# P V in 64x32 tiles over the live quarters, in two parts around a score set: a fused transformer block on one Trainium2 core

## The chip, the cores and the metric

The kernel runs on one core of one Trainium2 chip. The metric is the device time of one execution in microseconds (us), lower is better. The kernel before takes 324.31 us, the median of three runs (324.24 to 324.77).

## The reference, cut to what matters

One transformer block on 2048 tokens of width 640. Attention has 32 heads of 20 channels; every token sees itself and the 255 tokens before it. The second half is a gated MLP of width 1536. Both halves have a layer norm whose scale and shift, and a gate on the output, come from a small conditioning vector.

```python
mod = (_silu(c) @ w_mod).reshape(c.shape[0], 6, 1, -1)      # sa, ca, ga, sb, cb, gb
h = _layernorm(x) * (1 + ca) + sa
qkv = (h @ wqkv)                                            # 32 heads of 20, three times
scores = einsum('bhqd,bhkd->bhqk', q, k) * 20 ** -0.5
mask = (i - j >= 0) & (i - j < 256)
o = einsum('bhqk,bhkd->bhqd', softmax(where(mask, scores, -1e9)), v)
x = x + ga * (o @ wo)
h = _layernorm(x) * (1 + cb) + sb
x = x + gb * ((sigmoid(h @ w_gate) * (h @ w_up)) @ w_down)
```

## The kernel before, in words

The tokens are cut into 8 chunks `a` of 256 queries, each of two blocks of 128. For a chunk, the keys that can be live lie in four blocks of 128: two of the chunk before (`kb` = -2, -1) and two of its own (0, 1). The heads stand in 8 groups of 4; a step of attention, called (a, q) here, takes four groups `k` at once, so a chunk has two steps.

In a step TensorE (PE) first makes scores, keys on the partitions and queries on the columns. One *score set* fills the one PSUM tile S (4 banks of 512 columns, bank `j` for one of four heads). ScalarE (ACT) turns it into bf16 with one exponential (L981) in a tile E of SBUF; PE can write the next set only when that is done, since there is one S. GpSimd (POOL) then sets what is not live to zero with `affine_select` (L947). When all sets of a step are masked, PE does P V for the step: the *burst*, into two PSUM banks X. Column 20 of each head's V holds ones, so the sum of the softmax comes with it. VectorE (DVE) turns X (L1112, twice), divides, and at a chunk's second step turns the result into `oT`. Then come the output projection `wo`, the residual, the second layer norm, a DMA that transposes, the modulation, and the MLP (`wg`, `wu`, `wd`). Q and K get their transposed form `QT`, `KT` through DMAs as well (L769): projection on PE, copy out of PSUM into `stg` on ACT or DVE, DMA on SyncE's queue (SP).

Not every quarter of the scores is live. A quarter is 64 keys by 64 queries; of the 32 in a step's four key blocks 20 are, 8 of them cut by the diagonal. Two layouts stand beside each other:

- chunks 3 to 7 (merged): four main sets, one for each `k`, made of 20x64 tiles (half a key block each) so that two half blocks share a column, and one edge set for all `k` in 20x128 tiles. Five sets a step. `spread` masks and copies parts of a main set into the edge tile F, which takes two slots of E.
- chunks 1 and 2 (`WHOLE`): six sets a step of whole key blocks, in 20x128 tiles, masked in place. Chunk 0 has three sets a step.

A burst is 64 matmuls of 128x32 tiles (128 keys, 32 columns of V): for each `k` two of 256 columns and two of 128, each for four heads side by side in the array. It is issued together with a score set, straight ahead of it, as one operation (`both_of`).

Every instruction is an `op` with an engine, its reads and writes. The order on each engine, and which buffer an operation gets, stand as a list of numbers in the file (`PLAN`, `SLOTS`), made ahead of time; between engines the program waits by semaphores that follow from reads and writes. Engines run their lists strictly in order. Dense matmuls go through L634, tiled ones through L635.

Of the kernel before, what the change touches and what calls it, by code (L numbers as in the profile page):

```python
# [19 lines left out]
NG = H // 4  # L20
# [3 lines left out]
VW = 22  # L24
# [281 lines left out]
def c_pe(n):  # L306
# [132 lines left out]
MW = 64  # L439
NE = 8  # L440
ESI = 2
WHOLE = (1, 2)
WM1 = (3, 5)
AFTER = 1
NOW = 1
# [10 lines left out]
def build(nc, A_x, A_wqkv, A_wo, B_x, B_w_gate, B_w_up, B_w_down, c, w_mod, out, S=2048):  # L456
    NCH = S // CH
    P = Prog(nc)
    A = P.op
# [867 lines left out]
```

## Time and profile before

| | |
|---|---|
| median of three runs | 324.31 us |
| the profiled execution | 324.32 us, of which the span is 322.6 us |
| PE busy | 316.8 us, 98% of the span |
| ACT, DVE, POOL busy | 214.6, 199.9, 193.9 us |
| granted TensorE clock | full in all 40 slices |
| exponentials (L981) | 80, 1878 ns each |
| masks (L947) | 234, 149.3 us for the group that the page lists |

The span is what the profile covers; 1.7 us of the execution lie outside it. A row of the chain reads: start in us, duration, engine, tile written, line, number of instructions. The time of a row runs to the start of the next, so it holds what it costs to change over to the next kind of matmul. In a timeline row the duration runs to the end of the last instruction, which for pipelined matmuls lies well after the start of the next row; differences of starts are the better measure there. `128*32` is a tile of 128 rows and 32 columns in the array, `20*64` one of 20 rows and 64 columns.

### The profile page before, as it was taken

The page shows a single profiled execution, that of the slowest core. Times are in us where ns is not written, and L with a number is a line of the kernel's source. Part 1 is how long each engine was busy: PE and PEld are TensorE (multiplying, and loading weights), DVE is VectorE, ACT ScalarE, POOL GpSimd, SP SyncE. Part 2 cuts the span into 40 slices and gives each one's busy share as a digit, 9 for nine tenths or more (in the row PEclk, how much of TensorE's full clock was granted, in tenths as well). Part 3 has the DMA queues.
Part 4 walks back from the last instruction along what each step waited for, and adds up shares of the span by engine and source line. Part 5 has one row for each costly group of instructions (what it writes and reads, how often), then busy time and mean ns, then how long its engine had stood idle before and what let it go on. Part 6 is the DMA issues. An engine that isn't in the chain of part 4 may idle for free.

```text
span 322.6 us, 11139 instructions
## 1 busy us (share of the span) xinstructions
PE 316.8 (98%) x4766; PEld 230.9 (72%) x4766; DVE 199.9 (62%) x424; ACT 214.6 (67%) x220; POOL 193.9 (60%) x334
## 2 busy tenths in 40 slices
PE   6999999999999999999999999999999999999997
PEld 2666656577776677766787667876788777877885
DVE  6796999677585545685557454676438453485422
ACT  1489999997798787859785858684768557200320
POOL 4338679788788596969393839585672836601000
PEclk9999999999999999999999999999999999999999
DMA  7999799999912343308250211420400021012111
GB/s 231 374 332 199 198 258 206 184 273 317 210 40 41 103 92 48 62 3 130 55 114 4 35 35 48 102 43 2 122 6 4 2 43 43 2 41 43 41 43 42
DMA packets 64619, 33.61 MB, mean 104 GB/s; under 512 B 49082, under 2 KB 63034, under 8 KB 64570
## 3 DMA queue, kind: packets, MB, share of 16 engines
q1 hardware_dynamic: 63744, 31.92, 42.3%
q10 hardware_dynamic: 826, 0.98, 0.9%
q8 instruction: 37, 0.61, 0.8%
q14 instruction: 12, 0.10, 0.1%
HBM read 18.35 MB, written 2.62 MB: 65 GB/s over the span
## 4 chain that ended last, share of the span: by engine, by line
PE 89%; POOL 4%; ACT 3%; DVE 2%; DMA 1%; issue 1%; SPq 0%; ACTq 0%; DVEq 0%; POOLq 0%
PE M L634 74%; PE S L635 8%; PE M L635 7%; POOL E L947 3%; ACT E L981 2%; DMA x<-in_A_x_dram 1%; DVE x L762 1%; DVE st L741 1%; POOL st L749 1%; POOL st L747 0%; ACT QT L664 0%; DVE hT L823 0%; DVE st L743 0%; ACT hT L777 0%; SPq L533 0%
## 5 line engine op out<-in xcount | busy, mean ns | idle before, releaser
L947 POOL TENSOR_SCALAR_AFFINE_SELECT E<-E 128x256 bf16<-128x256 bf16 (+2 forms) x234 | 149.3, 667 | 52.2 <-ACT E L981 34.5
L981 ACT ACTIVATE E<-S 128x2048 bf16<-128x2048 f32 x80 | 150.2, 1878 | 42.3 <-PE S L635 41.6
L634 PE MATMUL M<-h2T,wu 128*128 128x256 bf16 x480 | 66.4, 273 | 0.0
L634 PE MATMUL M<-h2T,wg 128*128 128x256 bf16 x480 | 65.8, 273 | 0.0
L1225 DVE SCALAR_TENSOR_TENSOR hh<-sig,M 128x512 bf16<-128x512 f32 x48 | 32.4, 681 | 43.8 <-ACT sig L1223 31.6
L634 PE MATMUL M<-wd,hh 128*128 128x320 bf16 (+2 forms) x396 | 56.4, 295 | 0.0
L634 PEld LDWEIGHTS M<-h2T,wu 128*128 128x128 bf16 x480 | 45.7, 98 | 8.1 <-issue 1.6
L634 PEld LDWEIGHTS M<-h2T,wg 128*128 128x128 bf16 x480 | 45.5, 98 | 8.3 <-issue 1.5
L634 PEld LDWEIGHTS M<-wd,hh 128*128 128x128 bf16 x396 | 37.0, 98 | 14.9 <-issue 1.4
L1223 ACT ACTIVATE sig<-M 128x512 f32<-128x512 f32 x48 | 28.4, 596 | 26.1 <-PE M L634 25.0
L635 PE MATMUL S<-QT,KT 20*64 20x64 bf16 (+5 forms) x1600 | 33.3, 231 | 0.5
L1112 DVE STREAM_TRANSPOSE T<-M 128x512 f32<-128x512 f32 x32 | 21.7, 698 | 12.2 <-PE S L635 10.0
L741 DVE BATCH_NORM_STATS2 st<-x 128x6 f32<-128x320 bf16 x64 | 28.3, 477 | 1.1 <-DMA x<-in_A_x_dram 0.8
L635 PEld LDWEIGHTS S<-QT,KT 20*64 20x64 bf16 (+1 forms) x1600 | 15.2, 99 | 18.4 <-ACT E L981 9.8
L634 PE MATMUL M<-wk,hT 128*128 128x320 bf16 x160 | 28.2, 300 | 0.0
L634 PE MATMUL M<-wv,hT 128*128 128x320 bf16 x160 | 28.0, 300 | 0.0
L634 PE MATMUL M<-wo,oT 128*128 128x320 bf16 x160 | 26.5, 300 | 0.0
L634 PE MATMUL M<-wq,hT 128*128 128x320 bf16 x160 | 26.0, 300 | 0.2 <-DVE hT L823 0.2
L1244 DVE TENSOR_TENSOR x<-M,x 128x320 bf16<-128x320 f32 (+2 forms) x33 | 15.4, 478 | 15.1 <-PE M L634 14.5
L1179 DVE TENSOR_TENSOR x<-M,x 128x320 bf16<-128x320 f32 x32 | 15.3, 487 | 13.6 <-PE M L634 13.0
L747 POOL TENSOR_SCALAR st<-st 128x2 f32<-128x2 f32 (+1 forms) x17 | 4.0, 233 | 32.7 <-DVE st L743 31.7
L635 PEld LDWEIGHTS M<-E,V 128*32 128x32 bf16 x960 | 19.9, 97 | 4.5 <-issue 2.2
(81 smaller groups left out, 298.9 us busy)
## 6 DMA issues: line engine op xcount, KB each, us to landing
x<-in_A_x_dram SPq DMA_DIRECT2D x11, 320.0 KB, 3.6
wd<-in_w_mod_dram SPq DMA_DIRECT2D x6, 320.0 KB, 5.0
wd<-in_B_w_down_dram SPq DMA_DIRECT2D x4, 480.0 KB, 5.3
out_dram<-x SPq DMA_DIRECT2D x5, 320.0 KB, 2.6
wg<-in_B_w_gate_dram SPq DMA_DIRECT2D x2, 576.0 KB, 6.9
wu<-in_B_w_up_dram SPq DMA_DIRECT2D x2, 576.0 KB, 6.2
wu<-in_w_mod_dram SPq DMA_DIRECT2D x1, 960.0 KB, 10.5
wq<-in_A_wqkv_dram SPq DMA_DIRECT2D x2, 400.0 KB, 6.7
```

What stands on the lines that cost most here:

```text
L634: return e.matmul(o, l, r, start=st, stop=sp, skip_group_check=True)
L635: return e.matmul(o, l, r, start=st, stop=sp, tile_position=tp, skip_group_check=True)
L741: A("dve", lambda e, g, bi=bi, j=j: e.bn_stats(v(bi * 12 + j * 6, 6), src[bi].ap[:, j * 320:(j + 1) * 320]), 0.48, reads=[src[bi].r()], wr ...
L747: A("pool", lambda e, g, lo=lo, w=w: e.tensor_scalar(v(28 + lo, w), var()[:, lo:lo + w], EPS, None, op0=ALU.add), 0.2, reads=[st.r(("m", b ...
L749: A("pool", lambda e, g, lo=lo, w=w: e.tensor_tensor(v(30 + lo, w), v(28 + lo, w), mhalf[:, 0:w], op=ALU.pow), 0.71, reads=[st.r(("v", lo) ...
L947: return lambda e, eng: e.affine_select(dst(), src(), pattern=pattern, compare_op=ALU.is_ge, fill=0.0, base=base, channel_multiplier=mul)
L981: A("act", lambda e, eng: e.activation(dst(), src(Sp.ap), ACT.Exp, scale=SM_SCALE), 1.876, reads=[Sp.r()], writes=[E.r()], prio=3, tag=f"e ...
L1112: A("dve", lambda e, g, h=h: e.transpose(T1.ap[:, 512 * h:512 * h + 512], X[h].ap), 0.694, reads=[X[h].r()], writes=[T1.r(h)], prio=3.5, t ...
L1179: A("dve", lambda e, g, ps=ps, bi=bi, half=half: e.tensor_tensor(x1[bi].ap[:, half * 320:half * 320 + 320], ps.ap[:, 0:320], x1[bi].ap[:, ...
L1223: A("act", lambda e, g, pg=pg, sg=sg: e.activation(sg.ap[:], pg.ap[:], ACT.Tanh, scale=0.5), c_act(512), reads=[pg.r()], writes=[sg.r()], ...
L1225: A("dve", lambda e, g, pu=pu, sg=sg, f0=f0: e.scalar_tensor_tensor(out=hh.ap[:, f0:f0 + 2, :], in0=sg.ap[:].rearrange("p (a b) -> p a b", ...
L1244: A("dve", lambda e, g, ps=ps, bi=bi, c0=c0, n=n: e.tensor_tensor(x1[bi].ap[:, c0:c0 + n], ps.ap[:, 0:n], x1[bi].ap[:, c0:c0 + n], op=ALU. ...
```

## The change

1. **P V in 64x32 tiles over live quarters alone.** A piece is now half a key block (64 keys, partitions 0 to 63 or 64 to 127), and takes only the queries for which one of its quarters is live: for each `k` and head 1, 2, 3 or 4 quarters, 20 in all. A burst has 128 matmuls, of 256, 192, 128 and 64 columns, 32 of each. Matmuls of the lower and of the upper half alternate, lower with `k` 0 and 1 while upper has 2 and 3, so that the two write to different PSUM banks.
2. **In two parts.** `burst_halves` issues two operations; the second, with lower and upper swapped, waits on the first by a semaphore (`fence`). In the new order a score set, and at times dense matmuls, stand between the two.
3. **Merged sets in chunks 1 and 2 too** (`WHOLE = ()`): five sets a step in place of six, so 76 sets in all and not 80. The edge set is made of 20x64 tiles as well.
4. **Masks in place.** The edge tile takes one slot of E. Of a step's 18 masks 14 are on 64 partitions and four on 128. Where a mask on partitions 64 to 127 follows another instruction of POOL, or is followed by one, POOL waits for the one before (`part`); there are five such masks in a step.
5. **The order** is new from some 33 us on, on all engines, and with it which of ACT, DVE and POOL does some copies and modulations.

```diff
-WHOLE = (1, 2)
+WHOLE = ()
...
-    def score_set(a, q, si, tag, prods, low, E, dst, src, more=()):
+    def score_set(a, q, si, tag, prods, E, dst, src):
...
-            def both_of(e, eng):
-                pv(e, eng)
-                return sc(e, eng)
...
+        if pend and si == AFTER:
+            alone(*pend.pop(0))
...
+    def half_mask(a, E, key, g, t0, m, off):
+        hi, kind = key[:2] == "hi", key[2] == "A"
+        p0, p1 = (64, 128) if hi and kind else (0, 128) if hi else (0, 64)
+        ap = lambda: E.ap[p0:p1].rearrange("p j (t c) -> p j t c", c=g)[:, :, t0:t0 + m, off:off + 64]
+        mask(a, 256 * m, select(ap, ap, [[0, 4], [0, m], [-1 if kind else 1, 64]], -1 if kind else 64 * hi, 1 if kind else -1), [E.r()], [E.r(key)],
+             part="hi" if p0 else None)
...
     def edge_set(a, q, si):
-            prods += [(k, -2, 0, 128, 0, 64, 128 * k), (k, 1, 0, 128, 192, 64, 128 * k + 64)]
+            prods += [(k, 1, 0, 64, 128, 128, 128 * k), (k, -2, 64, 64, 0, 128, 128 * k)]
...
     def main_set(a, q, k, si):
-        prods = [(k, 1, 0, 64, 128, 64, 192), (k, -2, 64, 64, 64, 64, 256), (k, -1, 0, 64, 0, 192, 0), (k, 0, 64, 64, 64, 192, 320),
-                 (k, 0, 0, 64, 0, 256, 256), (k, -1, 64, 64, 0, 256, 0)]
+        prods = [(k, -2, 0, 64, 0, 64, 448), (k, 1, 64, 64, 192, 64, 256), (k, -1, 0, 64, 0, 192, 256), (k, 0, 64, 64, 64, 192, 320),
+                 (k, 0, 0, 64, 0, 256, 0), (k, -1, 64, 64, 0, 256, 0)]
+        half_mask(a, E, "loA", 64, 6, 2, 0)
+        half_mask(a, E, "hiB", 64, 4, 2, 0)
+        half_mask(a, E, "loB", 64, 0, 1, 0)
+        half_mask(a, E, "hiA", 64, 3, 1, 0)
...
-    def spread(a, q, k, E, F, fa):
...
+    def burst_halves(a, q, pieces):
+        o = None
+        for ph in range(2):
+            line = []
+            for p0 in (0, 64):
+                at = 0
+                for k in (2 * (ph ^ (p0 > 0)), 2 * (ph ^ (p0 > 0)) + 1):
+                    for p in sorted((p for p in pieces if p[0] == k and p[2] == p0), key=lambda p: KBO[p0].index(p[1])):
+                        line.append((at, p0, p))
+                        at += p[4]
+            line.sort(key=lambda x: x[:2])
...
+                        ins = mm(e, X[bank].ap[32 * j:32 * j + 32, oc:oc + n * 64], V[2 * a + kb].ap[p0:p0 + 64, h * VW:h * VW + 32],
+                                 ap(j), ph == 0 and (bank, j) not in seen, True, tp=(p0, 32 * j))
...
+            o = A("pe", pv, 0.55, reads=list(rd), writes=[x.r() for x in X], prio=8, lat=0.2, tag=f"pv{ph}_{a}", fence=o)
+        return X
...
+    KBO = {0: (0, -1, -2, 1), 64: (-1, 0, 1, -2)}
```

Three places show how the order moves, all on PE. The first is the first score set of chunk 1. `wk,hT1` is the K projection of chunk 1, `wv,hT1` its V projection, `KT0` and `KT1` are the transposed keys of chunks 0 and 1. Before:

```order
L634 MATMUL M<-wk,hT1 128x320 x5
L634 MATMUL M<-wv,hT1 128x320 x10
L635 MATMUL S0<-QT1,KT1 128x256 x4
L635 MATMUL S0<-QT1,KT0 128x256 x4
L634 MATMUL M<-grow,ident 128x160 x4
L634 MATMUL M<-wv,hT1 128x320 x5
```

And after:

```order
L636 MATMUL M<-wk,hT1 128x320 x5
L636 MATMUL M<-wv,hT1 128x320 x17
L636 MATMUL M<-grow,ident 128x160 x4
L636 MATMUL M<-wv,hT1 128x320 x3
L637 MATMUL S0<-QT1,KT0 64x64 x4
L637 MATMUL S0<-QT1,KT1 64x64 x4
L637 MATMUL S0<-QT1,KT0 64x192 x4
L637 MATMUL S0<-QT1,KT1 64x192 x4
```

The set stood behind ten matmuls and read the first key block of `KT1` alone; it now stands behind 24 and reads both, the second of which comes from the `wk` row at the top.

The second place is the first burst of chunk 1. Before:

```order
L634 MATMUL M<-wv,hT 128x320 x8
L635 MATMUL M<-E,V 32x256 x16
L635 MATMUL M<-E,V 32x128 x16
L635 MATMUL M<-E,V 32x256 x16
L635 MATMUL M<-E,V 32x128 x16
L635 MATMUL S<-QT,KT 128x256 x8
L634 MATMUL M<-wq,hT 128x320 x7
```

And after:

```order
L637 MATMUL M<-E,V 32x192 x8
L637 MATMUL M<-E,V 32x64 x8
L637 MATMUL M<-E,V 32x128 x8
L637 MATMUL S<-QT,KT 64x128 x32
L636 MATMUL M<-wq,hT 128x320 x13
L637 MATMUL M<-E,V 32x256 x8
L637 MATMUL M<-E,V 32x192 x8
L637 MATMUL M<-E,V 32x64 x8
```

One run of 64 matmuls ahead of a score set has become two runs of 64 (here the end of the first and the head of the second), with the edge set of the next step and 13 dense matmuls between.

The third place is in the same chunk, where two score sets stand close together. Before, behind the first burst:

```order
L635 MATMUL S<-QT,KT 128x128 x16
L634 MATMUL M<-wq,hT 128x320 x13
L634 MATMUL M<-wv,hT 128x320 x2
L635 MATMUL S<-QT,KT 128x256 x8
```

And after, ahead of it:

```order
L637 MATMUL S<-QT,KT 64x64 x8
L637 MATMUL S<-QT,KT 64x192 x8
L637 MATMUL S<-QT,KT 64x256 x8
L636 MATMUL M<-wq,hT 128x320 x11
L637 MATMUL S<-QT,KT 64x64 x8
```

Between one set and the next stood 15 dense matmuls; now there are 11.

More of the change, by code (lines that the diff above doesn't have):

```diff
@@ L966, in score_set, with mask @@
                 rd[QT[a].r((bi, q))] = 1
-        md = 3 if low else 1
-        now = pend.pop(0) if pend and si == AFTER else None
-        if now is None:
-            last["s"] = [A("pe", sc, 0.243, reads=list(rd), writes=[Sp.r()], prio=10, lat=0.2, tag=f"{tag}{a}",
-                           extra=last["s"], mode=md, hold=[E, *more])]
-        else:
-            pa, pv, pd, prd, X, hold = now[0]()
-            def both_of(e, eng):
-                pv(e, eng)
-                return sc(e, eng)
-            rd.update(prd)
-            last["s"] = [A("pe", both_of, pd + 0.09 + 0.243, reads=list(rd), writes=[Sp.r(), X[0].r(), X[1].r()], prio=10, lat=0.2,
-                           tag=f"pvs{pa}", extra=last["s"], mode=2, mout=md, hold=[E, *more, *hold, *X])]
-        A("act", lambda e, eng: e.activation(dst(), src(Sp.ap), ACT.Exp, scale=SM_SCALE), 1.876,
-          reads=[Sp.r()], writes=[E.r()], prio=3, tag=f"exp{a}", hold=more)
-        if now is not None:
-            now[1]()
-    def mask(a, n, fn, reads, writes, hold=()):
-        A("pool", fn, c_pool(n), reads=reads, writes=writes, prio=5, tag=f"mask{a}", hold=hold)
+        if pend and si == AFTER:
+            alone(*pend.pop(0))
+        last["s"] = [A("pe", sc, 0.243, reads=list(rd), writes=[Sp.r()], prio=10, lat=0.2, tag=f"{tag}{a}", extra=last["s"], hold=[E])]
+        A("act", lambda e, eng: e.activation(dst(), src(Sp.ap), ACT.Exp, scale=SM_SCALE), 1.876,
+          reads=[Sp.r()], writes=[E.r()], prio=3, tag=f"exp{a}")
+    def mask(a, n, fn, reads, writes, part=None):
+        A("pool", fn, c_pool(n) + (0.2 if part else 0.0), reads=reads, writes=writes, prio=5, tag=f"mask{a}", part=part)
     def first_sets(q):
@@ L1027, in edge_set @@
[L1027 to L1028 removed]
+        E = Tile(p_E, f"E{a}_{q}_4")
         prods = []
         for k in range(4):
[L1031 to L1035 removed]
@@ L1061, in sets @@
         if a in WHOLE:
-            return whole_sets(a, q)
-        F, fa, Es = None, None, []
+            return in_halves(whole_sets(a, q))
+        F, Es = None, []
         for si in range(5):
             if si == ESI:
-                F, fa = edge_set(a, q, si)
-                done = range(len(Es))
+                F = edge_set(a, q, si)
             else:
                 Es.append(main_set(a, q, len(Es), si))
-                done = [len(Es) - 1] if F is not None else []
-            for k in done:
-                spread(a, q, k, Es[k], F, fa)
@@ L1073, in sets @@
         out = []
+        fr = [F.r(), F.r("loB"), F.r("hiA")]
         for k, E in enumerate(Es):
[L1075 to L1080 removed]
@@ new lines, in sets, with in_halves, pv @@
+        return out
+    LIVE = {(-2, 0): (0, 1), (-1, 0): (0, 3), (0, 0): (0, 4), (1, 0): (2, 4), (-2, 64): (0, 2), (-1, 64): (0, 4), (0, 64): (1, 4), (1, 64): (3, 4)}
+    def in_halves(pieces):
+        out = []
+        for k, kb, u, n, ap, rs in pieces:
+            for p0 in (0, 64):
+                q0, q1 = LIVE[kb, p0]
+                out.append((k, kb, p0, q0, q1 - q0, lambda j, ap=ap, p0=p0, a0=q0 - 2 * u, a1=q1 - 2 * u: ap(j)[p0:p0 + 64, 64 * a0:64 * a1], rs))
+        return out
+    def burst_halves(a, q, pieces):
+        X = [Tile(p_M, f"O{a}_{q}x"), Tile(p_M, f"O{a}_{q}y")]
+        X[0].mate, X[1].mate = X[1], X[0]
+        o = None
+        for ph in range(2):
+            line = []
+            for p0 in (0, 64):
+                at = 0
[4 more added lines that the diff above has]
+            line.sort(key=lambda x: x[:2])
+            def pv(e, eng, ph=ph, line=line):
+                ins = None
+                seen = set()
+                for _, p0, (k, kb, _, u, n, ap, _) in line:
+                    bank = k // 2
+                    oc = (k % 2) * 256 + u * 64
+                    for j in range(4):
+                        h = NG * j + 4 * q + k
+                        ins = mm(e, X[bank].ap[32 * j:32 * j + 32, oc:oc + n * 64], V[2 * a + kb].ap[p0:p0 + 64, h * VW:h * VW + 32],
+                                 ap(j), ph == 0 and (bank, j) not in seen, True, tp=(p0, 32 * j))
+                        seen.add((bank, j))
+                return ins
+            rd = {}
+            for _, _, p in line:
+                rd.update(dict.fromkeys(p[6]))
+                rd.update(dict.fromkeys(V[2 * a + p[1]].r(h) for h in range(2)))
+            o = A("pe", pv, 0.55, reads=list(rd), writes=[x.r() for x in X], prio=8, lat=0.2, tag=f"pv{ph}_{a}", fence=o)
+        return X
@@ L1102, in burst @@
             rd.update(dict.fromkeys(rs))
-        for kb in range(-2 if a else 0, 2):
-            rd[V[2 * a + kb].r(0)] = 1
-            rd[V[2 * a + kb].r(1)] = 1
-        hold = list(dict.fromkeys(r.tile.mate for r in rd if r.tile is not None and r.tile.mate is not None))
-        return a, pv, sum(n for _, _, _, n, _, _ in pieces) * 128 / 2400.0 * 1.04 + 0.02, rd, X, hold
+        for kb in range(2):
+            rd[V[kb].r(0)] = 1
+            rd[V[kb].r(1)] = 1
+        A("pe", pv, sum(n for _, _, _, n, _, _ in pieces) * 128 / 2400.0 * 1.04 + 0.02, reads=list(rd), writes=[X[0].r(), X[1].r()],
+          prio=8, lat=0.2, tag=f"pvs{a}", hold=X)
+        return X
     def norm(X, Tn, oT, a, q):
@@ L1124, in norm, with alone @@
                   0.03 + 0.305 * (t1 - t0), reads=[Tn.r(0), Tn.r(1)], writes=[oT.r(t0 // 2)], prio=4, tag=f"tr2_{a}")
+    KBO = {0: (0, -1, -2, 1), 64: (-1, 0, 1, -2)}
     pend = []
-    def later(a, q, pieces, close):
-        made = []
-        def first():
-            made.append(burst(a, q, pieces))
-            return made[0]
-        return first, lambda: close(q, made[0][4])
-    def alone(first, then):
-        pa, pv, pd, prd, X, hold = first()
-        A("pe", pv, pd, reads=list(prd), writes=[X[0].r(), X[1].r()], prio=8, lat=0.2, tag=f"pvs{pa}", mode=2, hold=hold + X, extra=last["s"])
-        then()
+    def alone(a, q, pieces, close):
+        close(q, (burst_halves if a else burst)(a, q, pieces))
     def attention(a):
@@ L1152, in attention @@
             if a < NOW:
-                alone(*later(a, q, pieces, close))
+                alone(a, q, pieces, close)
             else:
-                pend.append(later(a, q, pieces, close))
+                pend.append((a, q, pieces, close))
     def add_pair(x, pss, prio, tag):
```

51 lines of the change are left out of this document (17 added, 34 removed), and 203 rows, old and new, of the table PLAN.

## The prediction

> **What bounds the kernel now.** First the shares and the chain on the page, then PE's own waits.
>
> ```profile
> PE 316.8 (98%) x4766; PEld 230.9 (72%) x4766; DVE 199.9 (62%) x424; ACT 214.6 (67%) x220; POOL 193.9 (60%) x334
> PE 89%; POOL 4%; ACT 3%; DVE 2%; DMA 1%; issue 1%; SPq 0%; ACTq 0%; DVEq 0%; POOLq 0%
> PE M L603 <- DMA c_row<-in_c_dram: 2.3, 1, 2.3
> PE M L635 <- POOL E L947: 0.2, 1, 0.2
> PE M L634 <- DVE hT L823: 0.2, 1, 0.2
> PE M L634 <- DVE x L762: 0.2, 1, 0.2
> ```
>
> PE is busy 98%, and of its 2.9 us of waits 2.3 are the start. So PE's own work sets the end: what PE is spared counts in full, what it newly waits for too, and time saved on ACT counts for nothing by itself. The sum is made against the profiled execution, 324.32 us (span 322.6 and 1.7 around it), 0.01 from the median of 324.31. About 0.2% (0.65 us) is what a measurement of this kernel can tell from no change.
>
> **What PE's work costs.** A dense stretch of the timeline, then pieces of the chain.
>
> ```profile
> 303.16 1.25 PE L634 MATMUL M<-h2T,wg 128*128 128x256 bf16 x10
> 304.25 0.82 PE L634 MATMUL M<-h2T,wu 128*128 128x256 bf16 x6
> ...
> 56.99 0.33 PE S L635 x8
> ...
> 106.84 0.36 PE S L635 x24
> 107.20 2.14 PE M L634 x15
> 109.35 0.34 PE S L635 x32
> ...
> 121.82 1.43 PE M L635 x64
> 123.25 0.36 PE S L635 x24
> ```
>
> Ten matmuls of 256 columns start in 304.25 - 303.16 = 1.09 us, so 0.109 for 256 columns; by columns 0.136 for 320, 0.082 for 192, 0.055 for 128, 0.027 for 64. Tiled matmuls run side by side, four or eight a round, or these rows could not be so short: 64 matmuls of a burst, 32 of 256 and 32 of 128 columns, are 16 rounds of four, 8 x 0.109 + 8 x 0.055 = 1.31 of the 1.43. A main set (8 matmuls each of 64, 192 and 256) is 0.027 + 0.082 + 0.109 = 0.22 of 0.36; an edge set, 8 rounds of 64, 0.22 of 0.34; a whole set, 2 rounds of 256, 0.22 of 0.33; 15 dense matmuls 2.04 of 2.14. What is left, 0.10 to 0.14, is the price of changing to the next kind of tile: 0.10 from dense, 0.11 to 0.12 from four in a round, 0.14 from eight.
>
> **The change, part by part.**
>
> *P V over live quarters.* One half has, lower beside upper, two groups `k` of one round each of 256, 192, 128 and 64 columns, eight matmuls in a round: 2 x 0.273 = 0.55. With a change at 0.12 (the burst's row, the same weights) to 0.14 (the main set's, eight in a round) it is 0.67 to 0.69, a burst of two 1.34 to 1.38 in place of 1.43. I take 0.67, since the main set's first round of 64 columns has no counterpart here: 14 bursts x 0.09 = -1.2 us, between -0.7 and -1.3. No 64x32 tile stands in the trace; the nearest thing with eight in a round is the main set. The Trainium skill, "TensorE: Matmul & The Clock Gate", Part 3, gives tiles side by side some 4 ns each after the first; as an estimate from that, eight end 16 ns later than four, which puts a half at 0.68 and the sum 0.4 us higher. The main set's 0.14 lies on that side.
>
> *Score sets.* Chunks 1 and 2 had 24 sets x 0.33 = 7.9; now 16 main x 0.36 + 4 edge x 0.34 = 7.1: -0.8. The ten edge sets of chunks 3 to 7 become four rounds of 128 in eights, 0.22 + 0.12 to 0.14: 0 to +0.2, taken as 0 with their own row.
>
> *Changes back from dense.* Counted over the order's rows, dense work is left 78 times where it was 81: -0.3. That a half is now a piece of its own is in its 0.67.
>
> So PE's work: -1.2 - 0.8 - 0.3 = -2.3 us.
>
> *The first score set of chunk 1.* It now reads both key blocks of its chunk.
>
> ```profile
> 32.26 1.52 PE L634 MATMUL M<-wv,hT 128*128 128x320 bf16 x10
> 32.50 0.45 DVE L665 CAST stg<-M 128x320 bf16<-128x320 f32 x1
> 32.98 1.23 SPq L769 DMA_TRANSPOSE KT<-stg  x1
> 33.71 0.40 PE L635 MATMUL S<-QT,KT 20*128 20x256 bf16 x8
> 34.04 0.45 PE L634 MATMUL M<-grow,ident 128*128 128x160 bf16 x4
> 34.33 0.84 PE L634 MATMUL M<-wv,hT 128*128 128x320 bf16 x5
> ...
> DMA to landing us min/median/max: 3.6/3.6/3.6
> ```
>
> The last row is that of the tile KT in this stretch. The second block's projection ends at 32.26, its copy at 32.95, its transpose is issued at 32.98 and lands at 36.6. None of this moves. PE does 20 `wv` matmuls (2.7) and the `grow` ones (0.29) first and reaches the set at 32.26 + 3.0 + 0.1 = 35.4. It then stands until 36.6: +1.25 us (0.9 if the landing is a few tenths quicker, 1.5 if copies slip). Behind it on PE stands everything; next in line is `wk` of chunk 2, which waits here although its input is there.
>
> *Sets closer than the exponential.*
>
> ```profile
> 52.12 0.36 PE S L635 x8
> 52.48 0.02 issue
> 52.51 1.89 ACT E L981
> 54.39 0.05 issue
> 54.44 0.40 PE S L635 x16
> ```
>
> With one S, a set can start 54.44 - 52.48 = 1.96 after the one before ended. Between the two sets of the third place lie 11 x 0.136 + 0.10 = 1.60: +0.36. By the same count three more pairs in the new order are 0.1 short, against two in the old one (this row, and one more): together +0.25 net.
>
> *Masks.* Of 252 masks of chunks 1 to 7, 196 are on 64 partitions, which no row shows.
>
> ```profile
> L947 POOL TENSOR_SCALAR_AFFINE_SELECT E<-E 128x512 bf16<-128x512 bf16 x112 | 70.8, 650 | 9.7 <-DVE wo L1272 3.0 <-ACT E L981 1.2 <-DVE x L762 1.0
> L947 POOL TENSOR_SCALAR_AFFINE_SELECT E<-E 128x1024 bf16<-128x1024 bf16 x40 | 44.9, 1135 | 16.4 <-ACT E L981 13.2 <-ACT V L664 1.7 <-DVE wd L1206 0.8
> L947 POOL TENSOR_SCALAR_AFFINE_SELECT E<-E 128x256 bf16<-128x256 bf16 x80 | 32.9, 424 | 25.7 <-ACT E L981 19.5 <-DVE x L762 2.2 <-DVE h2T L778 1.9
> L749 POOL TENSOR_TENSOR st<-st,mhalf 128x2 f32<-128x2 f32 x15 | 10.7, 712 | 0.9
> L754 POOL TENSOR_SCALAR st<-st 128x1 f32<-128x1 f32 x6 | 2.1, 366 | 0.4
> L1206 POOL TENSOR_TENSOR wd<-wd,gbc 128x640 bf16<-128x640 bf16 x5 | 6.9, 1394 | 1.8 <-DVE hT L778 1.2 <-DMA wd<-in_B_w_down_dram 0.5
> 280.00:322.60 42.60, 40.35 (x392) 32.39 (x389) 20.19 (x40) 6.37 (x11) 1.54 (x4) 1.00 0.14 40
> 101.44 3.86 POOL E L947 x5
> 105.30 0.04 issue
> 105.34 1.50 PE M L635 x64
> ```
>
> By columns, a step's masks cost 8 x 0.650 + 8 x 0.424 + 2 x 1.135 = 10.9, as merged steps did; a whole step's 9.7, so +4.5 us in chunks 1 and 2. Each of 70 masks on the upper half brings two waits of POOL on itself. L749, which always waits for POOL's instruction ahead, sat idle 0.9 / 15 = 0.06 for it: 140 x 0.06 = 8.4 us. Five `wd` products leave POOL (-7.0) and two of `wo` come (+2.8 at the same price). POOL goes from 194 to some 203, 63% of the span, and is no bound. What matters is a burst that comes before its last mask, as at 105.34 (PE waited 0.2). I counted for each burst the PE work between its last scores and itself against exponential (1.89) and masks in POOL's order: before, margins run from -0.3 to +1.1; after, from -0.4 to +4.3, with four below zero in place of two, while five have over 2 us. The nearest row is the one wait of 0.2, so I take 0, between -0.3 and +2 (a wait of 0.2 for each POOL change in the four tight bursts).
>
> *The fence and X.* The second half waits for the first. A score set (0.36) or dense work stands between in all but one burst, and covers it as the change of tile does; where the halves touch, the price is at least nothing and at most a few tenths: +0.1. X's two banks stay taken longer by what stands between, and dense chains have the other two; the tightest reuse of a bank by count is the same before and after.
>
> *Moved off the path.*
>
> ```profile
> wd<-in_w_mod_dram SPq DMA_DIRECT2D x1, 480.0 KB, 5.2
> ...
> 281.78 38.58 PE M L634 x324
> ```
>
> ACT loses four exponentials and 13 modulations or so, DVE gains some 5 us on 200; both stay under 65%. On SP the loads for the second conditioning product stand ahead of `wo`, `wg` and the fifth `x`; the product comes at about 43 us, and its last load, issued near 36, lands by 41.2 with the 5.2 of this load's row: 0, with 2 us in hand. The tail behind the last burst is 38.6 us of dense work, and is as long by count in the new order.
>
> New waits less the 0.2 at 105.34, where the margin is now 0.8: 1.25 + 0.25 + 0 + 0.1 - 0.2 = +1.4.
>
> **Sum:** 324.32 - 2.3 + 1.4 = 323.4 us.
>
> **The rivals.**
>
> *The waits eat it.* For this speaks that gain and new waits are of one size: with 0.14 for the change (+0.5) and four tight bursts late by 0.2 each, or 1.5 for the first set, the sum is 324.3. Against: the old order runs margins as tight almost without a wait. Not faster from 0.3 us more than I took.
>
> *POOL late (slower).* The place is the masks' last stretch ahead of a burst. If POOL has to run empty at each change of half, the price of one may be not 0.06 but the whole of a small instruction, L754's 0.37: 140 x 0.3 = 43 us more, POOL near 246 us, nearly all before 280 us, since behind it POOL works 1.54 us (the windows' row, its fifth busy time). A burst's last 11 masks hold about six changes, 1.8 us late, less margins of under 1 in eight of 14 bursts: 8 x 1.2 = +10, so 333. It decides from about 0.2 a change (0.8 x 4 bursts = +3, some 326). Only L749's 0.06 speaks against it.
>
> *The two halves take turns.* Each half then costs 0.55 more: 28 x 0.55 = +15, so 339. The main set's 0.36 for three rounds of eight speaks against it: there four row tiles write four banks at once. The Trainium skill, "TensorEngine Tiling (Array Packing)", Gotcha 1, says that row tiles must not use one PSUM bank at the same time and that software has to see to it; by that rule the halves run together as long as lower and upper are in different banks, as the order of `k` makes them, and this 339 is what it would cost otherwise. No run here shows it for accumulating matmuls.
>
> *More than forecast.* With the landing early, no mask late, and the main set's own change price at 0.12, 324.3 - 2.7 + 0.9 = 322.5.
>
> **How the numbers follow.** Forecast and "more" together 0.50 (321.4 to 323.7; the low end is PE's -2.3 with -0.6 more and no new wait), waits eat it 0.28 (323.7 to 324.95), POOL late 0.15, turns 0.04, other losses 0.03. Faster 0.51, with 0.01 of the rest; same 0.27; slower 0.22. The range runs from 321.4 to 325.6, where a weak case of POOL late still lies; a fifth is left out.
>
> **What would show it.** Right: halves of 64 matmuls at 0.65 to 0.70 in the chain, 0.36 for main sets, a PE wait of about 1.2 us near 36 us at a score set, released by a DMA to KT, PE busy near 315. Wrong: a half at 1.2 (turns); rows "PE M <- POOL E" of several tenths each, many times, and POOL waiting on POOL (POOL late); no wait near 36 us would leave a gain of over 2.

## The result, and the profile after

The changed kernel takes 336.85 us (median of four runs, 335.95 to 338.27) against 324.54 beside it: 1.038 times as long, 95% interval 1.034 to 1.043. The forecast was 323.4, and 325.6 was the top of its range. The profiled execution took 336.06 us.

The page of the changed kernel, its shares, its instruction queue (packets, MB, share) and its chain; the queue's row of the kernel before stands last:

```profile
PE 320.0 (96%) x5917; PEld 231.3 (69%) x5918; DVE 211.0 (63%) x435; ACT 202.5 (61%) x207; POOL 207.1 (62%) x356
q8 instruction: 46, 0.75, 1.0%
PE 79%; POOL 7%; DVE 5%; ACT 3%; issue 3%; DMA 2%; SPq 0%; POOLq 0%; DVEq 0%; ACTq 0%
```

```profile
q8 instruction: 37, 0.61, 0.8%
```

PE carries 79% of the chain where it carried 89%: it is waited for less and waits more. "Issue" has gone from 1% to 3%. PE runs 5917 matmuls, each with its own weight load, where it ran 4766, and 46 fetches of instructions come in where 37 did (the packets of `q8`). What PE waits for in the changed kernel (waits in total, times, longest):

```profile
PE M L636 <- issue: 2.7, 2, 2.0
PE M L605 <- DMA c_row<-in_c_dram: 2.6, 1, 2.6
PE M L637 <- issue: 2.5, 2, 2.0
PE M L637 <- POOL E L949: 1.1, 2, 0.6
PE S L637 <- ACT E L972: 0.6, 2, 0.4
PE S L637 <- DMA KT<-stg: 0.6, 1, 0.6
PE M L636 <- DVE stg L667: 0.4, 1, 0.4
PE M L636 <- DVE wo L1289: 0.3, 1, 0.3
```

Before, all waits but the start came to 0.6 us. Now 5.2 us of them have no releaser at all. The chain shows where two of these stand (start, duration, what):

```profile
56.80 0.40 PE M L637 x30
57.19 2.04 issue
59.23 0.51 PE M L637 x26
...
92.71 1.09 PE M L636 x9
93.80 2.03 issue
95.83 2.53 PE M L636 x11
...
163.54 0.75 PE M L637 x55
164.28 2.51 PE M L636 x22
166.79 0.74 PE M L637 x55
167.53 0.36 PE S L637 x24
```

The hole at 57 us lies inside one half of P V, among matmuls that one program step issues without any wait in it; the one at 93.8 between two `wu` matmuls. Neither of the instructions that go on behind the holes waits for a semaphore by its record, so neither hole shows as a wait for data (run 5 tests it). The last four rows show that a half takes 0.74 to 0.75, not 0.67, and a main set 0.36 as before. The row behind the second hole has a price of its own: 11 matmuls of 256 columns in 2.53 us, twice the usual 0.109 each. The windows around it (us; then PE, PEld, DVE, ACT and POOL busy, PEclk, DMA share, GB/s):

```profile
90.00:93.50 3.50, 3.50 (x111) 2.83 (x110) 2.89 (x7) 2.42 (x4) 0.00 (x0) 1.00 1.22 270
95.80:99.00 3.20, 3.17 (x36) 1.87 (x37) 2.67 (x5) 0.00 (x0) 3.06 (x5) 0.50 0.31 69
99.00:105.00 6.00, 6.00 (x92) 4.36 (x92) 5.84 (x15) 5.54 (x6) 3.90 (x7) 1.00 0.00 0
```

After the hole PE is granted half its clock for 3.2 us, which is 1.6 us lost. The Trainium skill, "TensorE: Matmul & The Clock Gate", Part 1, has the clock fall after an idle window of some 3.4 us. Here a hole of 2.3 us was enough once (granted clock 0.50 behind it), and at 57 us it was not. The four executions of the changed kernel had a mean granted clock of 1.00 (335.95 and 337.63 us) and 0.995 (336.06 and 338.27), so the half clock does not explain the difference between the two kernels.

**What the holes are.** I numbered PE's records (weight loads, matmuls, semaphore waits) in the order of their start and set them beside the starts of the transfers on the instruction queue, 16 KB each. Worked out from these records:

```
kernel         fetch starts   PE runs dry, after record   goes on at   hole   from fetch to going on
changed          56.88          56.98   1728 = 6 x 256 + 192   59.23    2.26    2.36
changed          71.73          73.23   2496 = 9 x 256 + 192   74.20    0.97    2.48
changed          93.21          93.53   3264 = 12 x 256 + 192  95.83    2.30    2.61
changed         219.79         221.74   8384 = 32 x 256 + 192  222.44   0.69    2.65
before, nearest 106.48         no hole                         111.27           4.78
```

So, by these records, PE reads its program in blocks of 256 instructions (46 x 256 is about its 11,900 records), asks for a block about when it goes over to the one ahead of it, and stands when it comes to the block's first instruction before it is there. At these four holes a block was there 2.4 to 2.7 us after its transfer started. After 100 us the start mostly lags about 1 us behind PE's going over (in dense stretches it comes up to 2.3 us ahead of it, so what asks for the block is not exactly the record's start); while weights load the lag is up to 4.2 us. A dense matmul of 256 columns and its load take 0.109 us, so 256 instructions last 14 us; half, edge set and half are 320 instructions in 1.85 us. The densest 256 records of PE took 3.8 us in the kernel before and 1.6 in the changed one.

The share of the DMA engines while the fetches of 56.88, 71.73 and 93.21 us were lagging, and in one lag of 1.6 us after 100 us:

```profile
53.80:56.90 3.10, 3.10 (x125) 2.07 (x118) 2.64 (x8) 2.51 (x4) 2.89 (x5) 1.00 0.97 248
69.80:71.70 1.90, 1.90 (x102) 1.36 (x103) 1.07 (x4) 1.38 (x1) 1.74 (x4) 1.00 1.06 301
89.00:93.20 4.20, 4.20 (x146) 3.41 (x135) 2.65 (x7) 3.12 (x4) 0.00 (x0) 1.00 1.21 245
197.40:198.90 1.50, 1.50 (x70) 1.16 (x49) 0.15 (x1) 1.50 (x2) 0.25 (x1) 1.00 0.00 0
```

The DMA engines are full (0.97 to 1.21) in the first three and idle in the last.

The Trainium skill, "Runtime: NRT & Kernel Launch", section Instruction fetch mechanics, says that instructions come in blocks of 16 KiB by a DMA queue of the sequencer's own. The trace agrees: each of the 46 transfers is 16 KB on a queue that carries nothing else. It also says that PE holds 2048 instructions and that crossing a block is mostly hidden. By the records PE ran dry with one block of 256 ahead, and the crossing was hidden in the kernel before but not in the changed one.

### The profile page after: what moved, and what is told of

Read it like the earlier page. It is cut to its first block, busy times and chain, and to the rows that moved or that the text cites. A ratio compares the mean times of both kernels' runs of the same rounds, so it can differ in the third digit from the quotient of the medians.

```text
span 334.3 us, 13466 instructions
## 1 busy us (share of the span) xinstructions
PE 320.0 (96%) x5917; PEld 231.3 (69%) x5918; DVE 211.0 (63%) x435; ACT 202.5 (61%) x207; POOL 207.1 (62%) x356
## 4 chain that ended last, share of the span: by engine, by line
PE 79%; POOL 7%; DVE 5%; ACT 3%; issue 3%; DMA 2%; SPq 0%; POOLq 0%; DVEq 0%; ACTq 0%
PE M L636 66%; PE M L637 7%; PE S L637 7%; POOL E L949 6%; ACT E L972 3%; DMA x<-in_A_x_dram 1%; DMA KT<-stg 1%; DVE st L743 1%; DVE wo L1289 1%; DVE oT L1149 1%; DVE x L764 0%; DVE hT L780 0%; DVE stg L667 0%; DVE T L1138 0%; POOL h2T L780 0%
## 5 line engine op out<-in xcount | busy, mean ns | idle before, releaser
L949 POOL TENSOR_SCALAR_AFFINE_SELECT E<-E 64x256 bf16<-64x256 bf16 (+5 forms) x258 | 165.5, 660 | 55.7 <-ACT E L972 33.1
L972 ACT ACTIVATE E<-S 128x2048 bf16<-128x2048 f32 x76 | 142.5, 1875 | 43.9 <-PE S L637 39.9
L636 PEld LDWEIGHTS M<-h2T,wg 128*128 128x128 bf16 x480 | 46.5, 98 | 7.7 <-issue 1.0
L636 PEld LDWEIGHTS M<-wd,hh 128*128 128x128 bf16 x396 | 36.9, 98 | 15.0 <-issue 1.7
L637 PE MATMUL M<-E,V 64*32 64x128 bf16 (+5 forms) x1856 | 24.9, 232 | 3.8 <-issue 2.5
L636 PE MATMUL M<-wk,hT 128*128 128x320 bf16 x160 | 27.1, 300 | 0.7 <-issue 0.7
L637 PEld LDWEIGHTS M<-E,V 64*32 64x32 bf16 (+1 forms) x1856 | 20.2, 90 | 10.1 <-issue 6.2
L636 PE MATMUL M<-wv,hT 128*128 128x320 bf16 x160 | 26.5, 300 | 0.1
L636 PE MATMUL M<-wo,oT 128*128 128x320 bf16 x160 | 25.4, 300 | 0.6 <-DVE stg L667 0.4
```

Source lines behind the costliest of these rows:

```text
L636: return e.matmul(o, l, r, start=st, stop=sp, skip_group_check=True)
L637: return e.matmul(o, l, r, start=st, stop=sp, tile_position=tp, skip_group_check=True)
L949: return lambda e, eng: e.affine_select(dst(), src(), pattern=pattern, compare_op=ALU.is_ge, fill=0.0, base=base, channel_multiplier=mul)
L972: A("act", lambda e, eng: e.activation(dst(), src(Sp.ap), ACT.Exp, scale=SM_SCALE), 1.876, reads=[Sp.r()], writes=[E.r()], prio=3, tag=f"e ...
```

## The experiments

Each ratio is against the kernel before, run beside it on the same chip (medians 324.8 to 325.9 there). The diffs are cut to what matters; `...` stands for what is left out, and helpers are written out in place.

**1. The halves alone, in the old order.**

```diff
             def both_of(e, eng):
-                pv(e, eng)
+                pv[0](e, eng)
                 return sc(e, eng)
...
+            A("pe", pv[1], 0.55, reads=list(prd), writes=[x.r() for x in X], ..., fence=last["s"][0])
```

> The kernel before, with P V of chunks 1 to 7 alone changed: two halves of 64x32 tiles over live quarters, the second behind the score set that follows the burst; every other instruction stands in the old order. Fetch theory (PE reads its instructions in blocks of 256, one block ahead, and a block that PE runs through in under some 3.5 us, or 5 to 7 us while the weights load, leaves it empty until the next has come): 28 halves x 0.745 less 14 bursts x 1.43 = +0.8 us, and 4 to 6 holes of 1 to 3 us named issue in the chain, each starting at an instruction of PE whose number leaves 192 when divided by 256; together +5 to +10, so 330 to 335. Rival, price of a half alone: +0.8 us, 325.3, no holes. Rival, the new order's waits are the cause: 324.5 to 325.5 here, since the old order stands. My prediction's price of a half (0.67): 323.3.

332.56 us, ratio 1.024 (1.020 to 1.029), inside the forecast of the fetch theory. Three holes of 0.75, 0.96 and 1.93 us (it had said four to six), after records that leave 192 or 193. But the second half waited for the score set too, since that stands in the op it waits for: set then half took 0.522 and 0.470 where the set alone takes 0.36 and 0.33, 2.0 us over ten and three places. So I repeated it.

**2. The same, the second half waiting for the first alone.**

```diff
+            o = A("pe", pv[0], ...)
+            last["s"] = [A("pe", sc, 0.243, reads=own, writes=[Sp.r()], ...)]
-            A("pe", pv[1], ..., fence=last["s"][0])
+            A("pe", pv[1], ..., fence=o)
```

> The run of the halves in the old order once more, with the second half waiting for the first alone and not for the score set between them (that wait cost 0.16 us at each of 13 places there: set then half 0.522 and 0.470 us where the set alone is 0.36 and 0.33). So 2.1 us less than 332.6 from that. Fetch theory: holes of together 3 to 6 us stay, at instructions whose number leaves 192; 328 to 331.5. Rival, price of a half alone (28 x 0.742 - 14 x 1.434 = +0.7): 325.3 to 326.3 without holes.

329.49 us, ratio 1.0135 (1.010 to 1.017): +4.4 us, with every other instruction in its old place; the rival without holes had 325.3 to 326.3. The chain through the largest hole:

```profile
141.33 0.36 PE S L611 x24
141.69 0.63 PE M L611 x45
142.32 1.78 issue
144.09 0.35 PE M L611 x16
144.44 2.14 PE M L610 x15
```

It is inside a half again, after record 18 x 256 + 193, and ends 2.64 us after the transfer of its block started. At 142 us no weights are loading (DMA share 0.02 from 138 to 146 us): PE went through the block ahead, which is half, score set and most of a half, in 1.5 us, and that is enough. The holes of this run come to some 4 us, the halves' price to 0.7. One wait in both runs has no explanation: 1.0 and 1.2 us near 35 us, ahead of any half, for a transpose into QT that landed in 4.4 to 4.9 us.

**3. The kernel before again**, unchanged, for that wait.

> The kernel before once more, for a second profile. In both runs of the halves in the old order PE waited 1.0 to 1.2 us near 35 us for a transpose into QT that landed 4.5 us after its issue, in the first profile of the kernel before it landed in 3.1 and nobody waited. If that landing varies from run to run, it is 4 to 5 us here in some case and the time is up to 1 us over 324.3; if the halves make it, it is 3.1 to 3.8 and nobody waits.

325.02 us. The transpose landed in 3.1 to 4.4 as before, and nobody waited for it. Why it is later with the halves in place stays open. This execution has a wait of PE of 0.9 us at 7 us, where the first profile has 0.2, ahead of everything that was changed. Runs 9 and 11 have it too (1.0 and 0.9), so differences of less than 1 us between runs say little.

**4. The new order with full tiles.**

```diff
-    for _, p0, (k, kb, _, u, n, ap, _) in line:            # 64 matmuls in 64x32 tiles
+    for k in (2 * ph, 2 * ph + 1):                          # 32 matmuls in 128x32 tiles
+        for kb, T, c0, oc, n in ((-1, Es[k], 0, 0, 256), (0, Es[k], 256, 0, 256), (-2, F, 128 * k, 0, 128), (1, F, 128 * k, 128, 128)):
```

> The changed kernel with each half of P V done as 32 matmuls in 128x32 tiles (8 of 256 columns and 8 of 128 for each of two groups) in place of 64 in 64x32 tiles; it reads the same tiles, in the same place of the order, but multiplies lower and upper rows by columns that don't belong together, so what it computes is not the attention. PE has some 1800 instructions fewer. Fetch theory: the holes of 57, 73, 93 and 222 us go (-6.2 us); a half is 0.655 of columns and 0.11 for the change, 0.75 to 0.77, as in the changed kernel: 330 to 331.5. Rival, order: the time stays at 336 to 337, since every wait of the new order stands. Rival, the halves' own rate is the cause: under 326.

333.03 us, ratio 1.024 (1.022 to 1.027), slower than the fetch theory's 330 to 331.5 and faster than the rival's 336 to 337. The four holes are gone (one of 0.7 came at 45 us), the densest 256 records take 3.6 us, and a half is 0.774. But only 3.8 us came back (4.7 with the 28 x 0.03 that these halves cost more), because other waits had stood in the holes' shadow. PE's waits in this run:

```profile
PE M L637 <- POOL E L949: 1.5, 3, 0.6
PE M L636 <- DVE V L667: 1.3, 1, 1.3
PE M L636 <- DVE h2T L780: 0.9, 1, 0.9
PE M L636 <- POOL hT L780: 0.7, 1, 0.7
PE S L637 <- ACT E L972: 0.6, 2, 0.4
PE S L637 <- DMA KT<-stg: 0.6, 1, 0.6
PE M L636 <- DVE hh L1244: 0.4, 1, 0.4
```

The five rows of POOL and DVE make 4.8 us, where the changed kernel has 2.0 us of such waits behind 30 us. So there is a second cause of about the same size in the rest of the change: the new order together with the merged sets and masks, which no run separates.

**5. Half a block of idle instructions ahead.**

```diff
-    for n in HEAT: zeros(n)
+    tiny(66)   # 66 matmuls of one column; three of the first five warming ones stay
+    for n in HEAT[1:]: zeros(n)
```

> The changed kernel with 128 more instructions of PE at its very start (66 matmuls of one column in place of two of the warming ones of 512), where PE only keeps warm. Fetch theory: the holes move in the program. They start again at instructions whose number leaves 192 when divided by 256, which are now 128 instructions earlier in the work, so not at the same matmuls as in the changed kernel (there inside the P V half at 57 us and between the wu matmuls at 93.5 us); the total of them is of the same size, 4 to 9 us, and the time 334 to 340. Rival, the holes belong to a place in the work (a wait on data that the trace doesn't show): they stay at the same matmuls, and the time is 336 to 337.

340.75 us, ratio 1.046 (1.041 to 1.051), just above the forecast. The holes moved: the largest, 2.81 us in the chain, now stands in a half at 92 us, where the changed kernel had none, and the `wu` chain behind it runs through.

```profile
89.20 2.29 PE M L633 x20
91.49 0.50 PE M L634 x33
91.99 2.81 issue
94.80 0.47 PE M L634 x17
```

The record is again 12 x 256 + 193, now 128 instructions earlier in the work. The rival, a place in the work, is out. The median is 3.9 us longer than the changed kernel's, so where the blocks' borders fall is worth something by itself. Of the 2.5 us between the two profiled executions the holes are 1.3 (7.6 us in sum), and waits on POOL and DVE grew too.

**6. The rounds of a half in falling widths.**

```diff
-    KBO = {0: (0, -1, -2, 1), 64: (-1, 0, 1, -2)}
+    KBO = {0: (0, -1, 1, -2), 64: (-1, 0, -2, 1)}
```

> The changed kernel with the rounds of each half in the order 256, 192, 128, 64 columns instead of 256, 192, 64, 128. If a half is bound by the rate at which PE takes up its 128 instructions (4.15 ns each in the second half of a half in the trace, 66 ns for a round of eight weights and eight matmuls), the last round ends 0.03 us sooner and a narrow round no longer stands between two wide ones: a half 0.71 to 0.72 instead of 0.745, -0.7 to -0.9 us in 28 halves, 336. If it is the columns alone and a dearer change of tile: 0.745 as it was, 336.9.

336.33 us (ratio 1.035, 1.031 to 1.039), a half 0.741: the order of widths does not matter. The rate of instructions had a half at 0.71 to 0.72, so this came out as the other reading said, columns and a dearer change of tile.

**7. Most columns of P V left out.**

```diff
-    X[bank].ap[..., oc:oc + n * 64], ..., ap(j)
+    w = 256 if n == 4 else 16
+    X[bank].ap[..., oc:oc + w], ..., ap(j)[:, 0:w]
```

> The changed kernel with every P V matmul of 64, 128 and 192 columns cut to its first 16 columns (the 256 wide ones stay), so that most products are left out; the number of PE's instructions is the same. A half then has 2 x 0.109 + 6 x 0.009 = 0.27 us of columns. If a half is bound by its 128 instructions (4.15 ns each): 0.53 and the change of tile, 0.63 to 0.74, as long as whole columns or nearly. If it is bound by columns: 0.27 + 0.19 = 0.46, and the time 8 us less before holes. Fetch theory: the holes at 57, 73, 93 and 222 us stay or grow, since the blocks are run through no slower.

335.1 us in two runs (1.031, 1.028 to 1.035). Half of the columns of a half are gone and it still takes 0.674: 0.28 us less streaming saves 0.07, so columns are not what bounds it here. That leaves its 128 instructions; but with run 6 neither instructions alone nor columns alone give the 0.742, and how the two add up stays open. The holes stay, 1.68, 0.65, 1.20 and 0.82 us at the same four records, and four of 0.3 to 0.4 come up beside them.

**8. Fewer bytes in the queues.**

```diff
-    wd[:, 3 * q:3 * q + 3, :]
+    wd[:, 3 * q:3 * q + 3, 0:32 if q < 3 else D]     # likewise the first part of each half of wu
```

> The changed kernel with five loads of weights (the first three quarters of wd and the first part of each half of wu, together 2.6 MB of the 13.3 MB that move between 36 and 100 us) cut to 32 columns; what stands there from before is used as weights in their place. Fetch theory: a fetch starts late because it stands behind these bytes (3 to 5 us after PE has gone over to the block ahead, against about 1 us after 100 us); with fewer bytes the fetches that started at 71.7 and 93.2 us start 1 to 3 us sooner, and the holes at 73 and 93.5 us (0.97 and 2.30) shrink to under 1 us together, while the one at 57 us, behind transposes and wg, may stay: 333 to 335.5. Rival, the lateness is a matter of PE's own queue: holes as they were, 336 to 337.5.

333.67 us, ratio 1.026 (1.022 to 1.029). The three fetches lag 1.0, 1.3 and 2.2 us where they lagged 3.1, 1.9 and 4.2, and the holes behind them are 0.60, 0.20 and 0.19 in place of 2.26, 0.97 and 2.30. So the loads make these fetches late; by what means, the trace does not show. I had thought that the hole at 57 us would stay; it shrank as the others did. The 4.5 us spared there became 3.2: other waits came up, as in run 4, and a new hole of 0.7 us at 46 us, where the loads are still whole.

**9 to 12. POOL and DVE in the new order.** In the full-tile kernel, products of `wo` and `wd` on 64 of 640 columns; then masks on a few columns in all chunks; then in chunks 1 and 2 alone; and the narrow masks once in the changed kernel itself.

```diff
-    e.tensor_tensor(wd[:, t, :], wd[:, t, :], gbc[:], op=ALU.mult)              # and wo
+    e.tensor_tensor(wd[:, t, 0:64], wd[:, t, 0:64], gbc[:, 0:64], op=ALU.mult)
-    E.ap[p0:p1]...[:, :, t0:t0 + m, off:off + 64]
+    E.ap[p0:p1]...[:, :, t0:t0 + m, off:off + 16]                                # m = 1 in main sets
```

> The run with P V in full 128x32 tiles in the new order (333.0), with the products of wo and wd by the gate done on 64 of their 640 columns, so that part of the output isn't scaled; DVE is spared 17 products of 0.5 to 1.3 us up to 107 us. Order theory, DVE late: of PE's waits there the ones that end on DVE near 49, 81, 100 to 105 us (together some 3 us) go or shrink to a third: 329.5 to 331. Rival, these waits come from elsewhere (transposes' landing, PE itself): 332.5 to 333.2.

330.31 us (1.016, 1.013 to 1.019): 2.7 us less than full tiles, inside the forecast. PE still waits 2.0 us on masks here, and on DVE 1.1 at 67 us and the 1.0 at 7 us.

> The run with P V in full 128x32 tiles in the new order (333.0), with each mask of chunks 1 to 7 done on a few columns alone (64 elements of a partition, 256 for the edge set, in place of 256 to 1024), so that most entries aren't masked; POOL is spared some 100 us. Order theory, POOL late: the waits of PE on POOL (67.6, 68.6, 194.7 and 231.7 us, together 2.5 us) go: 330 to 331. Rival, they are there in another form, or what follows is late by itself: 332.5 to 333.2.

327.18 us (1.007, 1.004 to 1.009): 5.9 us where the forecast was 2 to 3. With POOL's waits those on DVE went too, although nothing was taken from DVE's own work there. A hole of 1.2 us came at 58 us: full tiles don't keep every block from running dry.

> The run with P V in full tiles in the new order (333.0), with the masks of chunks 1 and 2 alone done on a few columns; the masks of chunks 3 to 7 are whole. Theory: the merged sets of chunks 1 and 2 put 53 masks of 33.9 us into 40 to 85 us, where the old order has 34 of 26.2 us, so that POOL has no idle time left there (42.2 of 45 us busy), and what stands on DVE up to 107 us comes late too. Then nearly all of the 5.9 us that narrow masks in all chunks brought comes from here, less the two waits of 0.6 us at 195 and 232 us that belong to chunks 5 and 6: 328 to 329.5. Rival, POOL's lateness is spread over the whole kernel (masks on 64 partitions, waits at each change of half): 330.5 to 332.

328.51 us (1.009, 1.006 to 1.011), inside the forecast: 4.5 of the 5.9 us come with the masks of chunks 1 and 2. The windows from 40 to 85 us, of the kernel before, the changed one, full tiles, and this run, in that order:

```profile
40.00:85.00 45.00, 44.82 (x602) 29.73 (x600) 35.54 (x79) 40.56 (x46) 36.90 (x53) 1.00 1.09 238
```

```profile
40.00:85.00 45.00, 41.10 (x900) 25.75 (x897) 35.64 (x76) 37.30 (x39) 41.02 (x69) 1.00 1.03 207
```

```profile
40.00:85.00 45.00, 42.11 (x782) 26.59 (x780) 36.59 (x79) 37.41 (x39) 42.16 (x69) 1.00 1.02 219
```

```profile
40.00:85.00 45.00, 44.41 (x841) 29.25 (x843) 35.48 (x85) 38.72 (x41) 27.39 (x75) 1.00 1.08 227
```

POOL (the fifth busy time) goes from 36.9 of 45 us to 41.0, and to 42.2 where no hole stops PE: little is left in which it could catch up. Narrow masks leave it at 27.4, far under the 36.9 of before. By mask rows, before and changed, in the same 45 us:

```profile
L947 POOL TENSOR_SCALAR_AFFINE_SELECT E<-E 128x512 bf16<-128x512 bf16 (+1 forms) x34 | 26.2, 798 | 5.9 <-ACT E L981 1.9 <-ACT V L664 1.7 <-DVE wd L1206 1.6
```

```profile
L949 POOL TENSOR_SCALAR_AFFINE_SELECT E<-E 64x256 bf16<-64x256 bf16 (+3 forms) x53 | 33.4, 654 | 2.9 <-ACT E L972 1.3 <-POOL st L756 0.2 <-POOL x L761 0.2
```

So the masks of these two chunks are what makes POOL late. Whether it is their number (53 for 34, 33.4 us for 26.2) or their closer place in the new order is not separated: no run has the old masks in the new order.

> The changed kernel (halves in 64x32 tiles) with each mask of chunks 1 to 7 done on a few columns alone, as in the run with full tiles and narrow masks; most entries aren't masked. Theory of two causes (holes of the instruction fetch, and POOL late from 40 to 85 us, where it is busy 41.0 of 45 us in the changed kernel and 36.9 before): what POOL's lateness costs goes, the holes stay, 5 to 8 us of them: 330.5 to 333. If the holes and POOL's lateness hide each other: 333 to 335. If POOL's lateness made the holes: 327 to 328, as with full tiles.

332.18 us, ratio 1.024 (1.017 to 1.032). The four executions run from 329.8 to 335.2, over the first two forecasts, so the time does not choose between them; the profiled one (329.76) does. PE's waits in it:

```profile
PE M L637 <- issue: 3.0, 2, 2.8
...
PE S L637 <- DMA KT<-stg: 0.6, 1, 0.6
PE S L637 <- ACT E L972: 0.6, 2, 0.4
PE S L637 <- issue: 0.3, 1, 0.3
```

All waits on POOL and DVE from 40 us on are gone, and holes of 3.0, 0.6, 0.3 and 0.4 us remain, 4.3 in all. So POOL does not make the holes, and by run 4 POOL is late without them. Side by side, in us:

| | all masks | narrow masks |
|---|---|---|
| halves in 64x32 tiles | 336.85 | 332.2 (329.8 to 335.2) |
| full tiles, same order | 333.0 | 327.2 |
| halves, old order | 329.5 | |
| before | 324.5 | |

Full tiles take away 3.8 us with all masks and 5.0 with narrow ones; narrow masks take away 4.7 us with halves and 5.9 with full tiles. So about 1 us of each cause stands in the other's shadow, which is less than the spread of the narrow-mask run; the trace shows it better (POOL and DVE 2.0 us in the changed kernel, 4.8 with full tiles). Narrow masks spare POOL more than the change had added, so their column is a bound and not a cure. No run came under the kernel before.

## Why the prediction was wrong, step by step

- *P V over live quarters, -1.2:* wrong by 1.9. The term took a half as 0.55 of columns and 0.12 for the change. It measured 0.742, 28 x 0.742 - 14 x 1.434 = +0.7 us, so the step that was mis-sized is the 0.12: it came to 0.19. Eight matmuls a round do run side by side, so the rival of the halves taking turns is out; but columns are not all that a half takes (run 7: still 0.674 with half of them). The main set, three rounds of 171 columns in the mean with 0.14 on top, did not show it; a half has eight rounds of 160.
- *A missing step, the instructions' own way in:* four holes of 6.2 us, counted from start to start, and 1.6 us at half clock behind one. The prediction counted tiles and columns of P V and never its instructions (64 more matmuls with 64 more loads per burst), though it had both counts. This is the largest error, and none of the prediction's rivals had it: that 333, POOL late, lies nearest to 336.85 is luck.
- *Masks, "63% of the span, and is no bound":* wrong. The prediction itself had +4.5 us of masks in chunks 1 and 2 and spread them over the span. In 40 to 85 us POOL had 8 us to spare and took 4.1 of it; with these masks narrow 4.5 us come back (run 11). The rival "POOL late" had the right engine and a wrong mechanism. It needed some 0.2 us at each change of half; POOL's idle time ahead of masks that is put down to its own masks is 0.2 us in all (the last row below), and gaps too short for the rows (under 0.15 us) sum to 7.1 us ahead of masks where they were 2.7, some 0.03 for each of 140 changes. The masks of chunks 3 to 7 cost 1.3 of the 5.9 us. The sum's 8.4 us for the changes of half came to about 4.4, and what it lacked instead is the size of masks on 64 partitions:

```profile
L949 POOL TENSOR_SCALAR_AFFINE_SELECT E<-E 64x256 bf16<-64x256 bf16 x112 | 52.1, 470 | 25.9 <-ACT E L972 13.2 <-DVE Tn L1142 8.0 <-DVE h2T L780 0.6
L949 POOL TENSOR_SCALAR_AFFINE_SELECT E<-E 64x512 bf16<-64x512 bf16 x56 | 38.4, 690 | 4.3 <-DVE x L764 1.9 <-DVE h2T L780 1.1 <-DVE V L667 0.2
L949 POOL TENSOR_SCALAR_AFFINE_SELECT E<-E 128x512 bf16<-128x512 bf16 x56 | 37.2, 671 | 10.9 <-ACT E L972 6.5 <-issue 1.6 <-DVE Tn L1142 1.0
L949 POOL TENSOR_SCALAR_AFFINE_SELECT E<-E 64x1024 bf16<-64x1024 bf16 x28 | 33.0, 1180 | 14.2 <-ACT E L972 12.9 <-POOL st L756 0.2 <-POOL E L949 0.2
```

  470, 690 and 1180 ns where 128 partitions took 424, 650 and 1135: 40 to 46 ns more, not less. A step's masks take 8 x 0.470 + 4 x 0.690 + 4 x 0.671 + 2 x 1.180 = 11.6 us where the sum had 10.9. POOL is busy 207 us.
- *Moved off the path, "DVE gains some 5 us", under 65%:* the share held (63%), the size did not (211.0 us for 199.9), and the reading is wrong for the same reason: a share over the span bounds nothing in one stretch. The products of `wd` now all stand on DVE, between 98 and 109 us, where seven of twelve stood there before 94 us. With full tiles narrow products gave back 2.7 us (run 9); in the changed kernel itself PE waits 0.9 us on DVE behind 30 us.
- *The first score set of chunk 1, +1.25:* right in place and releaser, wrong in size: 0.6, since the transpose landed in 3.05 us, not 3.6.
- *Sets closer than the exponential, +0.25:* 0.6 in two waits. *The fence, +0.1:* 0.2 at the one place where two halves touch (1.66 for both).
- *Score sets, -0.8:* right, 16 x 0.36 + 4 x 0.36 - 24 x 0.33 = -0.7; the ten later edge sets 0.36 for 0.345, +0.15.

Summed against the profiled run: 324.3 + 0.7 + 6.2 + 1.6 - 0.7 + 0.15 + 0.6 (KT) + 0.6 (ACT) + 1.1 (POOL) + 0.7 (DVE, the two rows shown) = 335.3 of 336.06. The term for changes back from dense, -0.3, is not in it: no row gives it by itself.

## What to carry to other kernels

Count instructions as well as columns: where tiles get smaller, find the densest 256 instructions of an engine and their time, and compare it with the fetch (here some 3.5 us from asking to having in quiet stretches, 4.4 to 6.8 at the three holes while weights load; the densest 256 took 3.8 us in the kernel before, 3.6 with full tiles and 1.6 with the halves). Read an engine's share in the stage where its work is added, not over the span. When two things make an engine wait in the same stretch, taking one away returns less than its row says, so take away each alone and then both.

## What the runs showed of the hardware

- A block of 256 instructions of PE was usable 2.2 to 2.9 us after its 16 KB transfer started, in 40 of the 41 holes of over 0.25 us that the traces of ten kernels here hold (once 3.5, where the transfer itself took 2.2 us). In the chain such a hole shows as "issue" and nothing else.
- 128 instructions of PE (64 loads, 64 matmuls in 64x32 tiles) took 0.742 us with 0.55 us of columns and still 0.674 with 0.27; in the second half of a half the starts stand 4 to 5 ns apart.
- PE's clock was halved for 3.2 us behind a hole of 2.3 us, but not behind the other one of 2.3, nor behind the 3.0 of run 12 and the 3.1 (2.8 in the chain) of run 5. The profiled execution of the kernel before was granted 1.00 in all slices.
